# A linear-attention and token-mixer kernel: in the second batch both K projections come before the outputs, Q's features lie in weights' homes, and the three parts of the weights' conversion are traced a block apart

## The chip, the cores and the metric

The kernel runs on one core of a Trainium2 chip. The metric is the time of one execution on the device in microseconds; lower is better. Three runs of the kernel before gave a median of 1150.87 us, from 1150.61 to 1150.98 us.

The engines are named as the profile names them: PE multiplies matrices, ACT and DVE work element by element on tiles, POOL does the 64-bit integer additions and the reductions over partitions, and SP issues the transfers between the chip's memory (HBM) and the on-chip memories SBUF and PSUM. [...] Each engine works through its own queue in order, and waits at an instruction until the semaphores that it names are set.

## The reference

Eight batches of eight heads with 576 rows of 64 numbers each go through linear attention with 128 features of each sign; the result, 576 rows of 512 numbers in each batch, goes through a mixer over rows (rank 32) and one over channels (512 to 2048 and back). The two weights w_ch1 and w_ch2, and U and V, come as 64-bit floating point; everything else is 32-bit.

```python
def phi(x):
    proj = np.einsum('bhsd,df->bhsf', x, w_phi)
    proj = proj - np.max(np.abs(proj), axis=-1, keepdims=True)
    return np.concatenate([np.exp(proj), np.exp(-proj)], axis=-1)
q_p, k_p = (phi(q), phi(k))
kv = np.einsum('bhsf,bhsd->bhfd', k_p, v)
z = np.sum(k_p, axis=2)
num = np.einsum('bhsf,bhfd->bhsd', q_p, kv)
den = np.einsum('bhsf,bhf->bhs', q_p, z)[..., None] + 1e-06
...
h = xt @ U @ V
u = x + h.transpose(0, 2, 1)
ch = np.maximum(u @ w_ch1, 0.0) @ w_ch2
return (u + ch).astype(np.float32)
```

## The kernel before

**Attention.** The heads are taken in pairs: a pair (b, j) is batch b and heads 2j and 2j+1, so there are four pairs in a batch. A pair's q and k are loaded (tiles `raw` for the 512 first rows, `t_r` for the last 64), transposed (`T`, `tail_T`), projected on the features (`pk` and `pkt` for K, `pq` and `pqt` for Q, all in PSUM), and turned into exponentials (`kp`, `kp_t`, `qp`, `qp_t`; `_t` marks the last 64 rows). `s_kv` sums K's features against v (`kv_ps`, then `kv`); `s_out` multiplies Q's features by that (`xpt`, `xp`) and divides, into `x` and, for the last 64 rows, `xt`. Batches 0 and 1 are transposed on PE, batches from 2 on by DVE. Three pairs are in flight: `cur` is at its outputs, `nxt` at its projections, `far` at its loading.

**Mixer.** Each batch has `pp`, `pst`, `vp` (the mixer over rows, into `x`), four transposes `pt` into `uT_hi` and `uT_lo`, and then 16 blocks of 128 hidden channels. Each block f has a first chunk, `hidden(f)` (12 matmuls into PSUM tile `ph`, then `h_hi` on ACT and `h_lo` on DVE), and a second chunk, `add(f)` (12 matmuls into `o`). `hidden(f+1)` stands ahead of `add(f)`. The chunks of one batch are laid between the attention steps of the next: each `pace.step()` emits one or two. The chunks of batch 0 thus run beside the attention of batch 1, which the change calls the second batch; it lies between about 90 and 235 us.

**The weights' conversion.** Each of the 16 blocks has two halves, one of w_ch1 and one of w_ch2, so there are 32 halves, numbered i. `load_weights` brings a block's 64-bit words, 0.5 MB for each half (`words`). `convert` makes 32-bit numbers of them: three operations on ACT (L143, L144, L146), a shift on DVE (L147) and an addition on POOL (L151), in one of four scratch buffers (`w_ab`). `split_w` then makes a leading part by a cast (L245; on ACT for w_ch1, on DVE for w_ch2) and a remainder by a subtraction on DVE (L246). `blocks(upto)` converts all halves up to a number, at every `pace.step()` by the line

```python
blocks(EARLY + steps[0] * (2 * NFC - EARLY) // CONVERT)
```

and at a chunk that needs a half which is still missing. It is needed for batch 0's chunks alone, since later batches find the weights converted. `made` holds the newest `h_hi`, behind which a conversion is placed by `issue_after`. Four blocks' converted weights (`STREAM`) are stored to HBM (`kept`) and read again by later batches.

**What sets the order.** PE's instructions stay in the order of the code. The other engines' and SP's queues are laid out by the framework, which places an instruction by a timeline of its own when it is traced; a conversion thus stands among the other work of ACT, DVE and POOL where that timeline had room. `LOADS` tells up to which block the weights are loaded with each of the first four pairs; `weights(LAST - 1)` and `weights(LAST)` load the rest. `q_features` lays Q's features of batch 0 and of pair (1,0) in SBUF homes of converted weights that do not exist yet (`w*_11`, `w*_12`).

## Time and profile before

| what | value |
|---|---|
| median of three runs | 1150.87 us |
| the profiled execution's own time | 1150.31 us |
| its span | 1148.5 us |
| mean granted clock of PE | 0.991 |
| ACT busy | 537.3 us, 47% |
| DVE busy | 672.1 us, 59% |
| POOL busy | 203.1 us, 18% |

The busy times are read from the first part of the page. The span is the time from the first to the last recorded instruction; the execution's own time is 1.8 us longer. The profile is one execution, so a sum made from its rows stands beside 1150.31 us, and the median of the runs is 0.56 us above that. In rows of the timeline, the number in square brackets is the idle time of that engine ahead of the row, with what ended it.

### The profile page before, as it was taken

To read this page: it belongs to the slowest core of one execution; us is meant where nothing else is said; L and a number is where in the kernel's file an instruction comes from. 1 tells how busy PE (TensorE), PEld (TensorE's weight loads), DVE (VectorE), ACT (ScalarE), POOL (GpSimd) and SP (SyncE) were. 2 spreads that over 40 slices of the span, in tenths; PEclk is the share of its full clock that TensorE was granted. 3 is DMA by queue.
4 is the path that set the end of the run, shared out by engine and by line. 5 is a ranking of instruction groups with operands and counts; after the bars stand their busy time and mean duration, and the time that the engine had idled before them with its cause. 6 is when DMAs were issued, how large, how long until landed. Compare 5 with 4: busy or idle time off the path is not lost.

```text
span 1148.5 us, 22126 instructions
## 1 busy us (share of the span) xinstructions
PE 1100.7 (96%) x8814; PEld 924.1 (80%) x8814; DVE 672.1 (59%) x1510; ACT 537.3 (47%) x1151; POOL 203.1 (18%) x154
## 2 busy tenths in 40 slices
PE   7877998899999999999999999999999999999998
PEld 6866876688887888888888888788888888888886
DVE  5767778656577656766667657765776434113111
ACT  6878787435553545354544554354535421111110
POOL 4434544201120112011111111011201200000000
PEclk8999999999999999999999999999999999999999
DMA  5995220322326233622353244413351126311101
GB/s 152 339 315 166 55 63 14 107 85 61 85 81 137 68 75 78 147 69 69 87 128 105 64 91 103 112 51 77 100 132 48 35 84 185 88 37 55 56 1 37
DMA packets 247047, 110.28 MB, mean 96 GB/s; under 512 B 211744, under 2 KB 224288, under 8 KB 246944
## 3 DMA queue, kind: packets, MB, share of 16 engines
q1 hardware_dynamic: 246624, 108.34, 35.7%
q8 instruction: 70, 1.15, 0.4%
q10 hardware_dynamic: 320, 0.52, 0.1%
q14 instruction: 33, 0.27, 0.1%
HBM read 86.80 MB, written 22.02 MB: 95 GB/s over the span
## 4 chain that ended last, share of the span: by engine, by line
PE 81%; DVE 6%; DMA 5%; ACT 4%; SPq 2%; issue 1%; POOL 1%; DVEq 0%; ACTq 0%; POOLq 0%
PE ph L77 31%; PE o L77 31%; PE kv_ps L77 6%; PE xp L77 4%; PE pq L77 3%; PE pk L77 2%; DMA words<-in_moe_w_ch_dram 2%; PE pp L77 1%; DVE w L246 1%; POOL w_ab L151 1%; DMA raw<-in_q_dram 1%; PE xpt L77 1%; PE vp L77 1%; DVE h_lo L688 1%; ACT w_ab L144 1%
## 5 line engine op out<-in xcount | busy, mean ns | idle before, releaser
L77 PE MATMUL ph<-uT_hi,w 128*128 128x512 f32 x1152 | 383.6, 394 | 6.0 <-DVE h_lo L688 6.0
L77 PE MATMUL o<-w,h_hi 128*128 128x512 f32 x1152 | 361.6, 395 | 0.0
L77 PEld LDWEIGHTS ph<-uT_hi,w 128*128 128x128 f32 x1152 | 216.3, 188 | 53.9 <-DVE h_lo L688 7.8
L77 PEld LDWEIGHTS o<-w,h_hi 128*128 128x128 f32 x1152 | 214.9, 189 | 45.1
L688 DVE SCALAR_TENSOR_TENSOR h_lo<-ph,h_hi 128x512 fp32r<-128x512 f32 x144 | 98.9, 687 | 244.0 <-ACT h_hi L687 243.4
L687 ACT ACTIVATE h_hi<-ph 128x512 fp32r<-128x512 f32 x144 | 85.6, 595 | 323.1 <-PE ph L77 322.8
L77 PE MATMUL o<-w,h_lo 128*128 128x512 f32 x576 | 225.9, 392 | 0.0
L77 PE MATMUL ph<-uT_lo,w 128*128 128x512 f32 x576 | 224.5, 390 | 0.0
L396 POOL PARTITION_ALL_REDUCE qp<-qp x64 | 128.5, 2014 | 247.4 <-ACT qp L395 247.4
L77 PEld LDWEIGHTS o<-w,h_lo 128*128 128x128 f32 x576 | 108.7, 189 | 23.3
L77 PEld LDWEIGHTS ph<-uT_lo,w 128*128 128x128 f32 x576 | 108.2, 188 | 20.9
L396 POOL PARTITION_ALL_REDUCE qp_t<-qp_t x32 | 25.7, 804 | 384.2 <-ACT qp_t L395 384.1
L348 DVE TENSOR_TENSOR T<-raw,T 64x512 fp32r<-64x512 f32 x96 | 70.9, 738 | 17.5 <-ACT T L347 15.0
L77 PE MATMUL kv_ps<-vb,kp 128*64 128x65 f32 x2048 | 68.5, 225 | 7.1 <-ACT kp L383 4.3
L77 PEld LDWEIGHTS kv_ps<-vb,kp 128*64 128x64 f32 x2048 | 63.4, 139 | 11.7 <-ACT kp L383 4.7
L398 ACT ACTIVATE qp<-qp 128x512 f32<-128x512 f32 x64 | 40.3, 630 | 66.1 <-DVE qp L397 65.9
L77 PE MATMUL xp<-kv,qp 128*64 128x65 f32 x2048 | 66.8, 224 | 3.9 <-ACT qp L399 3.7
L77 PEld LDWEIGHTS xp<-kv,qp 128*64 128x64 f32 x2048 | 63.8, 140 | 4.2 <-ACT qp L399 3.8
L347 ACT CAST T<-raw 64x512 fp32r<-64x512 f32 x96 | 59.3, 617 | 11.1 <-PE pq L77 9.9
L382 ACT ACTIVATE kp<-kp 128x512 f32<-128x512 f32 x64 | 40.4, 632 | 42.0 <-DVE kp L379 41.9
L151 POOL INT64_ADD w_ab<-w_ab x32 | 43.5, 1361 | 81.5 <-DVE w_ab L147 69.6
L397 DVE TENSOR_TENSOR qp<-qp 128x512 f32<-128x512 f32 x64 | 45.1, 705 | 19.3 <-POOL qp L396 18.9
(119 smaller groups left out, 1244.9 us busy)
## 6 DMA issues: line engine op xcount, KB each, us to landing
w<-kept SPq DMA_DIRECT2D x46, 512.0 KB, 3.7
words<-in_moe_w_ch_dram SPq DMA_DIRECT2D x32, 512.0 KB, 6.7
vb<-in_v_dram SPq DMA_DIRECT2D x64, 128.0 KB, 3.1
u_dram<-x SPq DMA_DIRECT2D x32, 256.0 KB, 2.9
st<-u_dram SPq DMA_DIRECT2D x16, 512.0 KB, 4.4
out_dram<-st SPq DMA_DIRECT2D x32, 256.0 KB, 2.1
y<-u_dram SPq DMA_DIRECT2D x56, 128.0 KB, 3.6
raw<-in_k_dram SPq DMA_DIRECT2D x96, 64.0 KB, 2.4
```

Source lines behind the costliest of these rows:

```text
L77: return tc.keep_in_program_order(nc.tensor.matmul(*args, **kw))
L144: nc.scalar.activation(out=bh.bitcast(F16)[:, :, 1], in_=f32(st[:, :, 1]), func=AF.Copy, scale=2.0 ** -60)
L151: nc.gpsimd.int64_add(a64, a64, b64)
L246: nc.vector.tensor_sub(w[:, 1, :], r, f32(w[:, 0, :]))
L347: nc.scalar.copy(out=m[here, s, :], in_=x_[here])
L348: nc.vector.tensor_sub(m[there, s, :], x_[here], f32(m[here, s, :]))
L382: nc.scalar.activation(out=kp[:, :, 0:F], in_=kp[:, :, F:2 * F], func=AF.Exp)
L396: nc.gpsimd.partition_all_reduce(qp[:, 0, :], qp[:, 1, :], P, ReduceOp.absmax)
L397: nc.vector.tensor_sub(qp[:, 1, :], qp[:, 1, :], qp[:, 0, :])
L398: nc.scalar.activation(out=qp[:, 0, :], in_=qp[:, 1, :], func=AF.Exp)
L687: on_act = nc.scalar.activation(out=h_hi, in_=ph, func=AF.Relu)
L688: on_dve = nc.vector.scalar_tensor_tensor(out=h_lo, in0=ph, scalar=0.0, in1=f32(h_hi), op0=ALU.max, op1=ALU.subtract)
```

## The change

It touches the first 240 us, up to the end of the second batch; from the third batch on, three small clearing instructions are left out and nothing else is moved.

- **Conversion.** `convert` is divided: `scale_words` (the three ACT operations), `add_words` (shift and addition), and `split_block` (cast and subtraction). `blocks` now takes one step at a time: it splits what is added, scales the next half, and adds the half before it. `CONVERT` goes from 21 to 24, so that the last halves come with later steps; what a chunk needs is completed by `splits(need)`.
- **Loads.** `LOADS` is (2, 4, 6, 8, 10) for five pairs, in place of (2, 5, 8, 10) for four. Blocks 11 to 15 are loaded behind the pairs' own loads, in three places.
- **Q's features.** Those of pairs (1,1) and (1,2) lie in the homes `w*_12` and `w*_14`.
- **K's projections.** For pairs (1,2) and (1,3), `s_project_k1` (the second K projection, and Q's for the last 64 rows) comes before `s_out` instead of behind it, and a bare `pace.step()` stands in its old place.
- **Small things.** `convert_uv` is called later in the first turn. `xt` is one tile for all batches, so its clearing (L938) at the end of every second batch is left out.

```diff
     def convert(st, name):
+        return add_words(*scale_words(st, name))
+
+    def scale_words(st, name):
...
         nc.scalar.activation(out=f32(a), in_=f32(st[:, :, 1]), func=AF.Abs, scale=2.0 ** -112)
+        return a, b_
+
+    def add_words(a, b_):
+
         nc.vector.tensor_scalar(
             out=a, in0=a, scalar1=3, scalar2=None, op0=ALU.logical_shift_left)
...
-    def convert_block(i):
+    def scale_block(i):
         f, n = divmod(i, 2)
-        r = convert(words[f][n], f"w{n + 1}_{f}")
+        found[i] = scale_words(words[f][n], f"w{n + 1}_{f}")
+
+    def add_block(i):
+        found[i] = add_words(*found[i])
+
+    def split_block(i):
+        f, n = divmod(i, 2)
         if f not in WHOLE:
             w = home.tile([P, 2, C], F32R, tag=f"w{n + 1}_{f}", name=f"w{n + 1}_{f}")
-            split_w((nc.scalar.copy, nc.vector.tensor_copy)[n], r, w)
+            split_w((nc.scalar.copy, nc.vector.tensor_copy)[n], found.pop(i), w)
...
-            if m == SM and (self.b == 0 or self.b == 1 and self.h0 == 0):
-                f = 11 + self.h0 // 2 % 2
+            lent = {0: (11, 12, 11, 12), 1: (11, 12, 14)}.get(self.b, ())[self.h0 // 2:]
+            if m == SM and lent:
+                f = lent[0]
...
-    loaded, converted = [0], [0]
+    loaded, scaled, added, ready = [0], [0], [0], [0]
...
-    def blocks(upto):
-        while converted[0] < min(upto, 2 * NFC):
+    def up_to(at, fn, upto):
+        while at[0] < min(upto, 2 * NFC):
             with ExitStack() as order:
 
                 for ins in made[-1:]:
                     for i in ins:
                         order.enter_context(tc.issue_after(i.ins))
-                convert_block(converted[0])
-            converted[0] += 1
+                fn(at[0])
+            at[0] += 1
+
+    def splits(upto):
+        up_to(added, add_block, upto)
+        up_to(ready, split_block, upto)
+
+    def blocks(upto):
+        while scaled[0] < min(upto, 2 * NFC):
+            splits(added[0])
+            up_to(scaled, scale_block, scaled[0] + 1)
+            up_to(added, add_block, scaled[0] - 1)
...
-                    blocks(2 * f + (2 if f == LAST or fn.__name__ == "add" else 1))
+                    need = 2 * f + (2 if f == LAST or fn.__name__ == "add" else 1)
+                    blocks(need)
+                    splits(need)
...
             mix(n)
+            splits(added[0])
...
-    LOADS = (2, 5, 8, 10)
-    EARLY, CONVERT = 5, 21
+    LOADS = (2, 4, 6, 8, 10)
+    EARLY, CONVERT = 5, 24
...
-        weights(LAST - 1)
+        with tc.issue_after(far.loaded.ins):
+            weights(11)
...
-        weights(LAST)
...
+            close = n > NPAIR + 2
             if nxt is not None and nxt.kp0 is None:
                 nxt.s_project_k0()
             pace.step()
+            if not close:
+                nxt.s_project_k1()
             pace.step()
             step(cur.s_out, x, xt)
-            if nxt is not None:
+            if not close:
+                with tc.issue_after(far.loaded.ins):
+                    weights((13, LAST)[n - NPAIR - 1])
+                pace.step()
+            elif nxt is not None:
                 step(nxt.s_project_k1)
...
-                    if b % 2 == 1:
-                        xt = moe.tile([P, C], F32, tag="xt", name=f"xt{b + 1}")
-                        nc.vector.memset(xt[ST:P], 0.0)
```

In the listings below the numbers at the ends of names are running numbers of tiles, and line numbers of the changed kernel are 12 to 13 higher than those of before at the same statement.

**SP, ahead of the loads of pair (1,1).** Before, this stands in SP's queue between the loads of pair (1,0) and the `t_r` of pair (1,1):

```order
59 L220 DMA words_1_738<-in_moe_w_ch_dram 128x4x256
60 L223 DMA words_2_739<-in_moe_w_ch_dram 128x1024
61 L316 DMA vb_91<-in_v_dram 128x4x64
62 L220 DMA words_1_742<-in_moe_w_ch_dram 128x4x256
63 L223 DMA words_2_743<-in_moe_w_ch_dram 128x1024
64 L220 DMA words_746<-in_moe_w_ch_dram 128x4x256
65 L223 DMA words_746<-in_moe_w_ch_dram 128x1024
66 L242 DMA kept_104<-w_0_723 128x1024
67 L305 DMA t_r_1_941<-in_k_dram 64x2x64
```

In the change the same place reads:

```order
53 L227 DMA words_1_728<-in_moe_w_ch_dram 128x4x256
54 L230 DMA words_2_729<-in_moe_w_ch_dram 128x1024
55 L328 DMA vb_91<-in_v_dram 128x4x64
56 L227 DMA words_1_732<-in_moe_w_ch_dram 128x4x256
57 L230 DMA words_2_733<-in_moe_w_ch_dram 128x1024
58 L317 DMA t_r_1_924<-in_k_dram 64x2x64
59 L304 DMA raw_1_0_920<-in_k_dram 128x2x256
60 L304 DMA raw_1_1_922<-in_q_dram 128x2x256
61 L317 DMA t_r_1_924<-in_q_dram 64x2x64
```

Counted from the loads of pair (1,0), 16 halves of words and one store to `kept` stood ahead of that `t_r` before, and 8 halves stand there now; block 8's words, the early ones of blocks 13 and 14, and the store are behind it.

**ACT, around `hidden(6)` of the second batch.** Before, these rows stand between `h_hi` of block 6 and of block 7:

```order
232 L687 ACTIVATE h_hi_6_1962<-ph_6_1949 128x512
233 L143 ACTIVATE w_9_ab<-words_2_949 128x512
234 L144 ACTIVATE w_9_ab<-words_2_949 128x512
235 L146 ACTIVATE w_9_ab<-words_2_949 128x512
236 L383 ACTIVATE kp_3_0_1903<-kp_3_0_1903 128x4x128
237 L245 CAST w_9_1946<-w_9_ab 128x512
238 L687 ACTIVATE h_hi_7_2055<-ph_7_2042 128x512
```

In the change, with `kp_3_1` the second K features of pair (1,3) and `qp_3_t` its Q features for the last rows:

```order
226 L394 ACTIVATE kp_3_1_1912<-kp_3_1_1912 128x4x128
227 L700 ACTIVATE h_hi_6_1945<-ph_6_1932 128x512
228 L146 ACTIVATE w_8_ab<-words_935 128x512
229 L395 ACTIVATE kp_3_1_1912<-kp_3_1_1912 128x4x128
230 L147 ACTIVATE w_8_ab<-words_935 128x512
231 L149 ACTIVATE w_8_ab<-words_935 128x512
232 L408 COPY qp_3_t<-pqt_3_1918 128x128
```

The K features stand ahead of block 6's `h_hi` now, the conversion there is at block 8 instead of 9, and the copy that empties `pqt`'s PSUM tile stands behind that conversion. On PE, `pqt_3` itself has moved from behind `hidden(7)` to just ahead of `hidden(6)`, and `xp_1_2`, the outputs of pair (1,2), come behind `hidden(6)` as before.

**ACT, ahead of the last block.** Before, between `h_hi` of blocks 14 and 15:

```order
334 L687 ACTIVATE h_hi_14_2728<-ph_14_2715 128x512
335 L382 ACTIVATE kp_1_0_2699<-kp_1_0_2699 128x4x128
336 L383 ACTIVATE kp_1_0_2699<-kp_1_0_2699 128x4x128
337 L687 ACTIVATE h_hi_15_2757<-ph_15_2744 128x512
```

In the change:

```order
327 L700 ACTIVATE h_hi_14_2706<-ph_14_2693 128x512
328 L146 ACTIVATE w_15_ab<-words_2046 128x512
329 L147 ACTIVATE w_15_ab<-words_2046 128x512
330 L149 ACTIVATE w_15_ab<-words_2046 128x512
331 L395 ACTIVATE kp_1_0_2677<-kp_1_0_2677 128x4x128
332 L146 ACTIVATE w_15_ab<-words_2046 128x512
333 L147 ACTIVATE w_15_ab<-words_2046 128x512
334 L149 ACTIVATE w_15_ab<-words_2046 128x512
335 L257 CAST w_2739<-w_15_ab 128x512
336 L700 ACTIVATE h_hi_15_2757<-ph_15_2744 128x512
```

And what DVE has behind `h_lo` of block 14 in the change:

```order
347 L701 SCALAR_TENSOR_TENSOR h_lo_14_2707<-ph_14_2693,h_hi_14_2706 128x512
348 L154 TENSOR_SCALAR w_14_ab<-w_14_ab 128x512
349 L154 TENSOR_SCALAR w_15_ab<-w_15_ab 128x512
350 L257 CAST w_14_2728<-w_14_ab 128x512
351 L258 TENSOR_TENSOR w_14_2728<-w_14_ab,w_14_2728 128x512
352 L154 TENSOR_SCALAR w_15_ab<-w_15_ab 128x512
353 L258 TENSOR_TENSOR w_2739<-w_15_ab,w_2739 128x512
354 L257 CAST w_2739<-w_15_ab 128x512
355 L258 TENSOR_TENSOR w_2739<-w_15_ab,w_2739 128x512
356 L701 SCALAR_TENSOR_TENSOR h_lo_15_2758<-ph_15_2744,h_hi_15_2757 128x512
```

The whole conversion of block 15, which was over by 211 us before, has moved between the last two `hidden` chunks. On PE only `add(13)` stands between those two.

## Prediction

> **What bounds the kernel now.** I read the engines' busy time first, then PE's waits in the first 260 us, since the change touches nothing behind 240 us but three clearings.

> ```profile
> PE 1100.7 (96%) x8814; PEld 924.1 (80%) x8814; DVE 672.1 (59%) x1510; ACT 537.3 (47%) x1151; POOL 203.1 (18%) x154
> ...
> PE tT L80 <- DMA t_r<-in_q_dram: 5.4, 2, 4.5
> ```

> The lower row gives an engine, the tile at which it waited, what it waited for, the total, the count and the longest wait in us. PE is busy for 96% of the span, and PE's work is the same before and after: the same rows, two pieces of them moved. So the time changes only where PE waits, and by the clock after a wait. The longest wait of the front ends on a transfer, and those of the second batch, which stand with their terms below, end on ACT or DVE. Two stretches show which engines are full there.

> ```profile
> 45.00:60.00 15.00, 12.01 (x184) 11.00 (x185) 10.24 (x29) 14.17 (x32) 6.81 (x6) 1.00 1.07 351
> 165.00:180.00 15.00, 9.68 (x67) 7.89 (x68) 13.00 (x21) 12.33 (x24) 8.75 (x6) 0.97 0.32 59
> ```

> The columns are the stretch, its length, the busy time of PE, PE's weight loads, DVE, ACT and POOL, the granted clock, the share of the DMA engines and GB/s. Up to 60 us the transfers are saturated; from 165 to 180 us PE is busy for 9.68 of 15 us beside DVE at 13.00 and ACT at 12.33. There, where a conversion stands in ACT's and DVE's queues decides what PE waits for.

> **The front: a gain.** The longest wait is for the `t_r` of pair (1,1).

> ```profile
> 63.13 0.63 SPq L305 DMA_DIRECT2D t_r<-in_q_dram  x1
> 70.26 0.45 PE L80 MATMUL tT<-ident,t_r 128*128 128x128 f32 x1 [4.47 <-DMA t_r<-in_q_dram]
> 70.50 1.91 PE L80 MATMUL T<-ident,raw 128*128 128x128 f32 x8
> 72.21 1.07 PE L77 MATMUL kv_ps<-vt,kp_t 128*128 128x130 f32 x4
> 96.82 1.04 PE L80 MATMUL T<-ident,raw 128*128 128x128 f32 x8
> 130.15 0.61 PE L77 MATMUL kv_ps<-vt,kp_t 128*128 128x130 f32 x4
> ```

> Eight halves and one store less stand ahead of these loads on SP. A half is 0.524 MB, 1.5 us at the 351 GB/s above, so they land some 9 x 1.5 = 13 us earlier, well ahead of the 65.8 us at which PE is ready (70.26 less 4.47). What goes is 4.47 of waiting, 0.87 in the eight transposes (1.91 against 1.04) and 0.46 in the next four matmuls (1.07 against 0.61): 5.8. What is late next are the splits of x on ACT and DVE that `pp` and `vp` need; they had lain in the shade of that wait. I give 0.6 back: **-5.2**, bounds -5.9 and -4.5.

> **Prices on ACT, DVE and POOL.** The rest comes from the order in these queues and from these rows.

> ```profile
> 108.71 0.64 ACT L398 ACTIVATE qp<-qp 128x512 f32<-128x512 f32 x1
> 109.24 0.62 ACT L382 ACTIVATE kp<-kp 128x512 f32<-128x512 f32 x1
> 109.76 0.61 ACT L245 CAST w<-w_ab 128x512 fp32r<-128x512 f32 x1
> 110.27 0.31 ACT L383 ACTIVATE kp_t<-kp_t 128x128 f32<-128x128 f32 x1
> 110.48 0.59 ACT L687 ACTIVATE h_hi<-ph 128x512 fp32r<-128x512 f32 x1
> 110.96 0.77 ACT L143 ACTIVATE w_ab<-words 128x512 uint16<-128x512 uint16 x1
> 111.59 0.76 ACT L144 ACTIVATE w_ab<-words 128x512 f16<-128x512 f32 x1
> 112.21 0.65 ACT L146 ACTIVATE w_ab<-words 128x512 f32<-128x512 f32 x1
> 112.75 0.63 ACT L399 ACTIVATE qp<-qp 128x512 f32<-128x512 f32 x1
> ...
> L246 DVE TENSOR_TENSOR w<-w_ab,w x28: 648/691/1728, 95.2 to 210.7; 128x512 fp32r<-128x512 f32 x28
> L151 POOL INT64_ADD w_ab<-w_ab x27: 1266/1292/1652, 96.6 to 208.4; - x27
> L147 DVE TENSOR_SCALAR w_ab<-w_ab x26: 396/420/1503, 100.8 to 207.9; 128x512 int32<-128x512 int32 x26
> L245 DVE CAST w<-w_ab x14: 412/428/1386, 99.6 to 209.7; 128x512 fp32r<-128x512 f32 x14
> ```

> On ACT, start to start, an exponential costs 0.53, a cast 0.51, a small exponential 0.21, an `h_hi` 0.48, and a half's three scalings 1.79 (110.96 to 112.75). On DVE a subtraction takes 0.69, a shift and a cast 0.42 each, on POOL an addition 1.29.

> **A new wait at `xp_1_2` (G).** This output goes to the PSUM bank that the copy of `qp_3_t` empties; before, that bank was filled only later. The stretch of PE from the end of `hidden(5)` to this output was:

> ```profile
> 140.49 0.38 PE L77 MATMUL pkt<-w_f,tail_T 128*128 128x128 f32 x2
> 141.38 0.81 PE L77 MATMUL o<-w,h_hi 128*128 128x512 f32 x2
> 147.40 2.04 PE L77 MATMUL xp<-kv,qp 128*64 128x65 f32 x64
> ```

> That is 6.9 us, and the second K projection with the small Q one, about as long as the first (140.49 to 141.38, 0.9), now stand in it: 7.8. ACT, from `h_hi_5` on, must do that `h_hi` 0.48, two halves 3.58, five exponentials, a cast and two small exponentials 3.58, then `h_hi_6` 0.48, three scalings with an exponential among them 2.32, and the small copy 0.27: 10.7 us. The difference, 2.9, is new; I take a little less, since an exponential may find its input early: **+2.7**, bounds 1.9 (two exponentials less) and 3.2.

> **Removed wait B and old waits A, C, D, E.**

> ```profile
> 113.43 1.04 PE L77 MATMUL xp<-kv,qp 128*64 128x65 f32 x28 [3.69 <-ACT qp L399]
> 115.84 1.05 PE L77 MATMUL o<-w,h_hi 128*128 128x512 f32 x2
> 134.37 0.62 PE L77 MATMUL o<-w,h_hi 128*128 128x512 f32 x2
> 166.33 1.04 PE L77 MATMUL kv_ps<-vb,kp 128*64 128x65 f32 x28 [2.10 <-ACT kp L383]
> 178.04 0.41 PE L77 MATMUL pkt<-w_hl,tail_T 128*128 128x128 f32 x2 [3.98 <-DVE tail_T L325]
> 207.78 0.34 PE L77 MATMUL kv_ps<-vb,kp 128*64 128x65 f32 x4 [2.88 <-ACT kp L382]
> 209.94 1.79 PE L77 MATMUL kv_ps<-vb,kp 128*64 128x65 f32 x28 [1.82 <-ACT kp L383]
> ```

> B, the 2.10 at 166 us, goes: the K features of pair (1,3) now stand ahead of `h_hi_6`, more than a block early: **-2.1**.

> A, the 3.69, stays. Its `xp` now waits for a division on DVE that stands behind `h_lo_2`, and ACT reaches `h_hi_2` 8.2 us after `h_hi_1` (0.48, two halves 3.58, and six exponentials, two small ones and a cast 4.1), against 7 to 7.5 us of PE: 3.1 to 4.9 in place of 3.69, so -0.6 to +1.2, taken as **+0.3**. Behind it the copy of `qp_2_1` stands behind three halves on ACT instead of two, 1.79 more, part of it covered: 0 to 1.2, **+0.6**. Block 8's first weights come as late as `hidden(8)`: 0 to 1.2, **+0.3**.

> C, the 3.98 for `tail_T`, stays. Its last copy on ACT now stands behind `h_hi_9` and four scalings of blocks 11 and 12: 0.48 + 1.79 + 0.6 and the copy and DVE's share of it, 0.8, are 3.7 us after `hidden(9)` at the least. With every DVE subtraction on the way stretched it is 7.3: 0 to +3.3, taken nearer to the plain rows, **+1.5**. D, a small wait for the copy of `qp_t` near 199 us, loses 0 to 0.8 by the same queue, **+0.4**. E, 4.70 in two pieces, stands behind blocks 13 and 14 on ACT as it stood behind 14 and 15: 3.7 to 5.8, -0.9 to +1.1, **+0.1**.

> **A new wait at the last block (F).** Only `add(13)` stands on PE between `hidden(14)` and `hidden(15)`, 2.8 us by the twelve matmuls of the chunk in the rows below (229.45 to 232.30). The whole of block 15 is converted there. Counted from the end of `hidden(14)`: `h_hi` and `h_lo` to 1.4, the shift of `w_14`'s second half to 1.8, its addition to 3.1, cast and subtraction to 4.2; this frees the scratch buffer that block 15's second half waits for; its scalings run to 6.1, and the cast and the subtraction of the first half, behind them in ACT's and DVE's queues, to 7.3. PE waits 7.3 - 2.8 = 4.5. The wait at the same place before goes with its cause.

> ```profile
> 225.55 0.48 DVE L938 MEMSET xt<- 64x512 f32 x1 [4.37 <-DMA u_dram<-xt]
> 229.45 0.50 PE L77 MATMUL ph<-uT_hi,w 128*128 128x512 f32 x1 [0.83 <-DVE h_lo L688]
> 232.30 1.47 PE L80 MATMUL pt<-ident,x 128*128 128x128 f32 x12
> ```

> The clearing waited 4.37 us for a transfer and made `h_lo` late, 0.83 on PE. So 4.5 - 0.8 = **+3.7**; bounds 2.9 (the buffer free 0.9 earlier) and 4.9 (one subtraction stretched). The other two clearings have no wait behind them: 0. PE's slow clock after the wait is a term of its own. After 3.69 a pair of `o` matmuls took 1.05 instead of 0.62, for four such pairs, some 1.6 us in all with the single ones; after 2.10 and below nothing is seen. For 4.5 that is 0 to 1.6, **+0.8** taken as the middle, since the transposes behind `hidden(15)` have slack.

> [...]

> **The sum.** -5.2 + 2.7 - 2.1 + 0.3 + 0.6 + 0.3 + 1.5 + 0.4 + 0.1 + 3.7 + 0.8 = **+3.1**. On the profiled execution's 1150.3 that is 1153.4, and by its 0.56 below the median, **1154.0**: slower by 0.27%. All low ends give -4.7 (1146), all high ends +11.9 (1163).

> **Rivals.**

> *The lag works, and the kernel is faster.* The casts wait for POOL now.

> ```profile
>   ACT w L245: 4.9, 5
>   DVE w L245: 8.6, 6
> ```

> The rows are who waited for an addition between 95 and 235 us, how long and how often. With cast and subtraction a block behind, those 4.9 us on ACT go. If all of it reaches PE at A, C and E instead of my +1.9 there, the sum is 3.1 - 1.9 - 4.9 = -3.7, 1147; if also the queue ahead of the last block is one half shorter (1.8 less at F), 1145. It decides from where ACT's lost time stands ahead of those waits and neither DVE nor the end of a `ph` is later; five waits of 1 us, over 140 us, seldom stand so. 0.18.

> *The last block isn't late.* If `w_15` is converted ahead of `hidden(14)` after all, F and its clock go: 1154.0 - 4.5 = 1149.5, no change. Against it stands the order on ACT. 0.14.

> *The load gain fails.* If the loads of pair (1,1) are held by another tile than the queue, the 5.2 stay: 1159.2. The saturated DMA share speaks for little of that. 0.07.

> *Subtractions meet additions.* One beside an addition took long:

> ```profile
> 107.11 1.67 DVE L246 TENSOR_TENSOR w<-w_ab,w 128x512 fp32r<-128x512 f32 x1
> 106.92 1.32 POOL L151 INT64_ADD w_ab<-w_ab  x1 [0.51 <-DVE w_ab L147]
> ```

> 1.67 is 0.98 over the median. With the parts apart, a subtraction stands beside the next half's addition more often; one at each of A, C, E and F makes +3.9, 1157.9. 0.16. [...]

> **How the numbers follow.** My forecast has 0.45, between 1149.5 and 1157. A measurement of this kernel can tell some 0.2% (2.3 us) from no change: below 1148.6 is faster, above 1153.2 slower. Faster: 0.16 of the first rival, 0.04 of the second, 0.07 of the forecast, 0.27. Slower: 0.07 and 0.15 of the last two, 0.23 of the forecast, 0.01 of the second: 0.46. The rest is 0.27. For 8 in 10 the range reaches into the first rival and over the last two: 1145 to 1160.

> **What would show it.** PE should wait for no `t_r` near 65 us, and its first `ph` should come at 88 to 89 us instead of 93.75. A wait of 2 to 3 us should stand at an `xp` behind `hidden(6)`, none at `kv_ps` after it, and one of 3 to 5 us at the last `ph` of the second batch, ended by a subtraction on DVE. The forecast is wrong if the waits for `tail_T` and for the last K features are gone: then ACT's and DVE's queues hold less than I counted.

## The result, and the profile after

The changed kernel takes 1162.38 us (median of four runs, 1162.31 to 1163.85) beside 1150.74 us for the kernel before in the same runs: a ratio of 1.0107, with a 95% interval of 1.009 to 1.0125. The forecast was 1154.0 us in a range of 1145 to 1160: the direction is right, and the loss is 11.6 us where 3.1 were forecast.

Where it lies is read from three stretches of each execution: up to the first `ph` of the first mixer, from there to the first `ph` of the next one, and the rest. These are the rows of before, with the columns as in the prediction (stretch, its length, busy time of PE and of the others, clock, DMA share, GB/s).

```profile
0.00:93.75 93.75, 74.20 (x989) 63.47 (x990) 65.43 (x177) 67.95 (x154) 36.30 (x46) 0.95 0.86 269
93.75:239.58 145.83, 128.64 (x930) 106.55 (x928) 107.28 (x204) 105.01 (x207) 57.59 (x40) 0.96 0.25 66
239.58:1148.50 908.92, 897.89 (x6899) 754.03 (x6897) 499.36 (x1130) 364.35 (x791) 109.21 (x69) 1.00 0.33 83
```

And these are the same stretches of the changed kernel.

```profile
0.00:90.44 90.44, 75.75 (x989) 65.20 (x990) 65.49 (x174) 66.90 (x152) 36.59 (x45) 0.92 0.78 244
90.44:252.06 161.62, 133.52 (x930) 109.68 (x929) 111.51 (x207) 106.14 (x209) 60.09 (x41) 0.90 0.29 79
252.06:1160.60 908.54, 897.54 (x6899) 754.43 (x6897) 498.36 (x1128) 364.01 (x791) 109.26 (x69) 1.00 0.33 83
```

The counts of matmuls agree, so the stretches hold the same work. The third is unchanged. In the front PE waits 14.7 us (90.44 - 75.75) instead of 19.6, and is busy 1.6 us longer for the same 989 matmuls: 3.3 gained. In the second batch it waits 28.1 instead of 17.2 and is busy 4.9 us longer: 15.8 lost. Of the whole difference of 12.1 us in the span, **6.0 are waiting and 6.1 are the same matmuls at a lower clock** (mean granted clock 0.981, before 0.991).

The waits in PE's timeline, at the places that the prediction named A, G, C, D, E and F (start, duration, engine, line, operation, and the idle time ahead with its end):

```profile
110.10 1.15 PE L77 MATMUL xp<-kv,qp 128*64 128x65 f32 x32 [3.06 <-DVE xt L507]
147.21 1.15 PE L77 MATMUL xp<-kv,qp 128*64 128x65 f32 x32 [2.10 <-ACT qp_t L408]
159.57 0.74 PE L77 MATMUL ph<-uT_hi,w 128*128 128x512 f32 x2 [1.48 <-DVE w L258]
178.38 0.66 PE L77 MATMUL pkt<-w_hl,tail_T 128*128 128x128 f32 x2 [7.09 <-DVE tail_T L337]
200.78 1.22 PE L77 MATMUL pq<-T,w_hl 128*128 128x512 f32 x2 [2.03 <-ACT qp_t L408]
210.31 0.34 PE L77 MATMUL kv_ps<-vb,kp 128*64 128x65 f32 x4 [1.58 <-ACT kp L394]
213.63 1.78 PE L77 MATMUL kv_ps<-vb,kp 128*64 128x65 f32 x28 [2.98 <-ACT kp L395]
238.33 0.79 PE L77 MATMUL ph<-uT_hi,w 128*128 128x512 f32 x1 [5.63 <-ACT w L257]
240.08 1.22 PE L77 MATMUL ph<-uT_hi,w 128*128 128x512 f32 x2 [0.53 <-DVE w L258]
```

Each wait stands where the prediction put it: the new one at `xp` behind `hidden(6)` (2.10), none at `kv_ps` behind it, block 8's weights (1.48), `tail_T` (7.09, before 3.98) and the last block (5.63 and 0.53, before 0.83). The two in the chunk of block 15 come from these rows of DVE, in which a conversion's shift is L154, its cast L257 and its subtraction L258:

```profile
232.61 0.97 DVE L154 TENSOR_SCALAR w_ab<-w_ab 128x512 int32<-128x512 int32 x1 [0.78 <-ACT w_ab L149]
233.50 0.41 DVE L257 CAST w<-w_ab 128x512 fp32r<-128x512 f32 x1
233.95 1.63 DVE L258 TENSOR_TENSOR w<-w_ab,w 128x512 fp32r<-128x512 f32 x1
237.60 0.43 DVE L154 TENSOR_SCALAR w_ab<-w_ab 128x512 int32<-128x512 int32 x1 [2.02 <-ACT w_ab L149]
238.31 1.72 DVE L258 TENSOR_TENSOR w<-w_ab,w 128x512 fp32r<-128x512 f32 x1 [0.28 <-ACT w L257]
```

and from these of ACT (the row that waits for DVE) and POOL:

```profile
235.67 0.78 ACT L146 ACTIVATE w_ab<-words 128x512 uint16<-128x512 uint16 x1 [2.58 <-DVE w L258]
...
232.02 1.28 POOL L158 INT64_ADD w_ab<-w_ab  x1 [11.52 <-DVE w_ab L154]
233.75 1.28 POOL L158 INT64_ADD w_ab<-w_ab  x1 [0.45 <-DVE w_ab L154]
238.20 1.28 POOL L158 INT64_ADD w_ab<-w_ab  x1 [3.17 <-DVE w_ab L154]
```

The subtraction at 233.95 frees the scratch buffer; it began 0.2 us behind an addition on POOL and took 1.63 instead of 0.69, so ACT started the last half's scalings at 235.67, 0.9 later than without. The next subtraction, at 238.31, met an addition too, which is the second wait of 0.53.

### The profile page after: what moved, and what is told of

Same layout as the page of the kernel before. It is cut to its first block, busy times and chain, and to the rows that moved or that the text cites. A ratio compares the mean times of both kernels' runs of the same rounds, so it can differ in the third digit from the quotient of the medians.

```text
span 1160.6 us, 22131 instructions
## 1 busy us (share of the span) xinstructions
PE 1106.8 (95%) x8814; PEld 929.3 (80%) x8814; DVE 675.4 (58%) x1507; ACT 537.0 (46%) x1151; POOL 205.9 (18%) x154
## 3 DMA queue, kind: packets, MB, share of 16 engines
q8 instruction: 70, 1.15, 0.4%
## 4 chain that ended last, share of the span: by engine, by line
PE 85%; DVE 6%; ACT 5%; SPq 1%; DMA 1%; issue 1%; POOL 1%; ACTq 0%; POOLq 0%; DVEq 0%
PE ph L77 32%; PE o L77 32%; PE kv_ps L77 6%; PE xp L77 5%; PE pq L77 3%; PE pk L77 3%; PE pp L77 1%; DVE w L258 1%; PE xpt L77 1%; ACT w_ab L146 1%; PE vp L77 1%; ACT w_ab L147 1%; ACT h_hi L700 1%; DVE h_lo L701 1%; ACT w_ab L149 1%
## 5 line engine op out<-in xcount | busy, mean ns | idle before, releaser
L77 PE MATMUL ph<-uT_hi,w 128*128 128x512 f32 x1152 | 386.8, 397 | 12.7 <-ACT w L257 5.6
L77 PE MATMUL o<-w,h_hi 128*128 128x512 f32 x1152 | 360.8, 395 | 0.0
L77 PEld LDWEIGHTS ph<-uT_hi,w 128*128 128x128 f32 x1152 | 217.9, 189 | 61.4 <-ACT w L257 6.1
L77 PEld LDWEIGHTS o<-w,h_hi 128*128 128x128 f32 x1152 | 214.6, 189 | 44.7
L77 PE MATMUL ph<-uT_lo,w 128*128 128x512 f32 x576 | 226.2, 393 | 0.0
L77 PE MATMUL o<-w,h_lo 128*128 128x512 f32 x576 | 225.6, 392 | 0.0
L77 PEld LDWEIGHTS o<-w,h_lo 128*128 128x128 f32 x576 | 108.7, 189 | 23.3
L77 PEld LDWEIGHTS ph<-uT_lo,w 128*128 128x128 f32 x576 | 109.2, 190 | 21.1
L77 PE MATMUL xp<-kv,qp 128*64 128x65 f32 x2048 | 68.5, 227 | 5.6 <-DVE xt L507 3.1
L77 PE MATMUL kv_ps<-vb,kp 128*64 128x65 f32 x2048 | 68.2, 225 | 4.7 <-ACT kp L395 3.1
L77 PEld LDWEIGHTS kv_ps<-vb,kp 128*64 128x64 f32 x2048 | 63.3, 139 | 9.0 <-ACT kp L395 3.4
L77 PEld LDWEIGHTS xp<-kv,qp 128*64 128x64 f32 x2048 | 65.3, 143 | 6.0 <-ACT w_ab L149 3.2
```

The costliest lines, as they stand in the source:

```text
L77: return tc.keep_in_program_order(nc.tensor.matmul(*args, **kw))
```

## The experiments

Each kernel was timed against the kernel before on the same chip; ratios are to that, with their 95% intervals. The changed kernel's own ratio is 1.0107 (1.009 to 1.0125), and 0.1% is 1.15 us.

| kernel | what differs from the change | ratio (95%) |
|---|---|---|
| c21 | CONVERT 21 | 0.9968 (0.9949 to 0.9986) |
| c23 | CONVERT 23 | 0.9926 (0.9905 to 0.9947) |
| nolag | no lag between the parts | 0.9979 (0.9967 to 0.9992) |
| nolag21 | no lag, CONVERT 21 | 1.0004 (0.9991 to 1.0017) |
| nolag23 | no lag, CONVERT 23 | 0.9939 (0.9924 to 0.9953) |
| loads_only | no lag, CONVERT 21, K's projection late | 0.9958 (0.9945 to 0.9972) |
| k1late_c21 | CONVERT 21, K's projection late | 0.9970 (0.9957 to 0.9983) |
| nolag23_k1late | no lag, CONVERT 23, K's projection late | 0.9916 (0.9885 to 0.9947) |
| oldloads_c21 | CONVERT 21, loads and homes of before | 1.0042 (1.0026 to 1.0059) |
| gate | conversion placed behind `tail_T` | 1.0044 (1.0028 to 1.0059) |
| busy | useless matmuls in one wait | 1.0076 (1.0058 to 1.0094) |
| fill | useless matmuls in three waits | 1.0066 (1.0051 to 1.0081) |

**The pace and the lag.** The first question was which of the two puts the conversion late.

```diff
-    EARLY, CONVERT = 5, 24
+    EARLY, CONVERT = 5, 21
```

> The change with CONVERT at 21 again, so that block 15's halves are scaled at earlier steps; all else as in the change. Theory P (pace): the late pace alone puts block 15 between the last two hidden chunks, and of the 12 us lost some 8 are the wait there (5.6 and 0.5, less 0.8 before) and the slow clock behind it; expected: a wait of at most 1.5 us at the last ph, no slow matmuls there, 1153 to 1156 us. Theory L (lag): the parts of the conversion that are traced a block apart are what is late, at every block; expected: the casts and subtractions still come late, at most 3 us gained, over 1159 us.

Measured: 0.9968, the wait at the last `ph` gone, and a mean granted clock of 0.987 in the profiled execution, in the change 0.981. That is theory P, but the gain of some 16 us (1.4%) is about twice what it gave. Read at the starts of the same `ph` tiles, the last block is 9.5 us of it; 7 us more come earlier, 4.7 of them between the starts of blocks 9 and 10, where the wait for `tail_T` is 3.30 instead of 7.09.

```diff
     def blocks(upto):
         while scaled[0] < min(upto, 2 * NFC):
-            splits(added[0])
             up_to(scaled, scale_block, scaled[0] + 1)
-            up_to(added, add_block, scaled[0] - 1)
+            splits(scaled[0])
```

> The change with each half scaled, added and split at one step, CONVERT still 24. Theory P: block 15 is still converted between the last two hidden chunks, wait there 4 to 7 us and slow matmuls behind; within 4 us of the change, 1158 to 1163 us. Theory L: the waits for tail_T (7.1), qp_t (2.0) and the last ph go back to those of before; below 1154 us.

Measured: 0.9979, against both expectations in part. Theory P had it within 4 us of the change; it gained 15. Theory L had the last wait go; it stays, at 2.92 us, with slow matmuls behind:

```profile
225.30 0.79 PE L77 MATMUL ph<-uT_hi,w 128*128 128x512 f32 x1 [2.92 <-ACT w L257]
225.89 0.63 PE L77 MATMUL ph<-uT_lo,w 128*128 128x512 f32 x1
```

Without the lag block 14's second half is split ahead of `h_hi` of block 14, so its buffer is free, and the last wait is half as long. The wait for `tail_T` is 4.52 instead of 7.09, the one for block 8's weights is gone, and those for `kp` are 2.12 instead of 4.56 (at D it waits 2.28 instead of 2.03). So the lag and the pace each do most of the harm only beside the other.

The kernel with both edits, CONVERT 21 and no lag:

> The change with each half converted at one step and CONVERT at 21, so that the loads, the homes of Q's features and K's order are all that is left of it. Theory P and theory L both: the conversion is as before, so the wait at the last ph is under 1 us; what is left is the front (-3.3), the removed wait for kp (-2.1) and the new one at xp (+2.1): 1146 to 1150 us. If the order of K's projections or the loads were what costs, it stays above 1155 us.

Measured: 1.0004, above the 1146 to 1150 us that was expected. The wait at the last `ph` is gone, as expected, but at `xp` PE waits 4.37 and 3.35 us, more than in the change (3.06 and 2.10). That K's early projection is what costs more there, with the conversion ahead again, is shown by the later run loads_only, which takes that projection out and leaves the rest.

One number apart from the change, and the sharpest test of its pace:

```diff
-    EARLY, CONVERT = 5, 24
+    EARLY, CONVERT = 5, 23
```

> The change with CONVERT 23 in place of 24 and nothing else: the last half is scaled with the last step of the second batch, ahead of hidden(13). Theory P (the pace of one number puts block 15 between the last two chunks): no wait over 1 us at the last ph and no slow clock behind it, which were worth 9 us; the waits at tail_T (7.1) and qp_t (2.0) are a matter of how many halves are still left there and shrink by 0 to 3 us: 1.000 to 1.003 of before. Theory L (it is the lag): the casts of block 15 still come behind h_hi of block 14; over 1.006 of before.

Measured: 0.9926, better than expected: 1.8% by one number, by the two ratios (18.7 us between the profiled executions). There are 23 steps in the second batch, so at 24 the last two halves are left for the last chunk, which must complete them at once. By the starts of the same `ph` tiles 9.5 of 18.8 us lie at the last block and 8.2 at the wait for `tail_T`:

```profile
172.96 0.41 PE L77 MATMUL pkt<-w_hl,tail_T 128*128 128x128 f32 x2 [1.38 <-DVE tail_T L337]
...
223.22 0.39 PE L77 MATMUL ph<-uT_hi,w 128*128 128x512 f32 x1
```

The last `ph` has no idle time ahead of it. That `tail_T` waits 1.38 instead of 7.09 was not expected of the pace. ACT's order shows how: with 23 both copies of `tail_T` stand ahead of `h_hi` of block 9.

```profile
171.06 0.24 ACT L336 CAST tail_T<-tT 64x128 fp32r<-64x128 f32 x1
172.22 0.26 ACT L336 CAST tail_T<-tT 64x128 fp32r<-64x128 f32 x1 [0.92 <-DVE tail_T L337]
172.51 0.60 ACT L700 ACTIVATE h_hi<-ph 128x512 fp32r<-128x512 f32 x1
```

In the change the second copy stands behind `h_hi`, and DVE's second subtraction for it follows a long one beside POOL:

```profile
172.15 0.59 ACT L700 ACTIVATE h_hi<-ph 128x512 fp32r<-128x512 f32 x1
...
173.62 0.28 DVE L337 TENSOR_TENSOR tail_T<-tT,tail_T 64x128 fp32r<-64x128 f32 x1
...
173.89 0.64 ACT L149 ACTIVATE w_ab<-words 128x512 f32<-128x512 f32 x1
174.43 0.77 ACT L146 ACTIVATE w_ab<-words 128x512 uint16<-128x512 uint16 x1
175.22 0.26 ACT L336 CAST tail_T<-tT 64x128 fp32r<-64x128 f32 x1
...
175.81 1.77 DVE L258 TENSOR_TENSOR w<-w_ab,w 128x512 fp32r<-128x512 f32 x1
177.50 0.41 DVE L154 TENSOR_SCALAR w_ab<-w_ab 128x512 int32<-128x512 int32 x1
177.94 0.29 DVE L337 TENSOR_TENSOR tail_T<-tT,tail_T 64x128 fp32r<-64x128 f32 x1
```

Here the copy at 175.22 comes 3.1 us behind `h_hi`, past four scalings. It waits for DVE's first subtraction, as the row at 172.22 above shows, and that ended at 173.90: so of the 3.1 us the scalings cost it 1.3, from 173.90 on. DVE reaches the second subtraction at 177.94, 2.5 us after the copy's end. Beside c23, where neither takes any time, and with the first subtraction 2.0 us later in the chunk of block 9, that makes the 5.7 us more. The next run forces the other order on the change, by placing each piece of the conversion behind the newest `tail_T`:

```diff
-            nc.vector.tensor_sub(dst[D:2 * D], src, f32(dst[0:D]))
+            gate[:] = [nc.vector.tensor_sub(dst[D:2 * D], src, f32(dst[0:D]))]
...
                     for i in ins:
                         order.enter_context(tc.issue_after(i.ins))
+                for i in gate:
+                    order.enter_context(tc.issue_after(i.ins))
                 fn(at[0])
```

> The change with each scaling and split of the conversion placed behind the newest subtraction of tail_T, so that both copies of tail_T stand ahead of h_hi of block 9 and of the scalings of blocks 11 and 12 on ACT. Theory Q (the wait of 7.1 us for tail_T is made by these scalings and by the split beside POOL's addition): that wait is at most 3 us, and 4 us or more of it stay gained up to hidden(10); the last block stays late (5 to 6 us); 1.003 to 1.008 of before. Rival: T's own splits on DVE end as late; the wait stays over 5 us and the time at 1.009 or more; or the conversion behind the gate is what comes late instead, at ph of block 10.

Measured: 1.0044, and

```profile
172.80 0.65 PE L77 MATMUL pkt<-w_hl,tail_T 128*128 128x128 f32 x2 [2.05 <-DVE tail_T L337]
...
180.40 0.74 PE L77 MATMUL ph<-uT_hi,w 128*128 128x512 f32 x2 [1.86 <-DVE w L258]
```

The wait falls from 7.09 to 2.05, which theory Q expected; 1.86 of it come back at block 10, whose weights are now behind the gate, which the rival named. At the start of block 11 some 4 us are kept (187.9 against 192.2 in the change), of which 0.5 were there before block 9. Another 3.9 us come between the starts of blocks 12 and 13, at the waits for `kp`, and no run tells why. The last block stays late, at 5.66 us.

**Loads and K's order.** These take the other parts of the change alone.

```diff
-            if not close:
-                nxt.s_project_k1()
             pace.step()
...
                     weights((13, LAST)[n - NPAIR - 1])
-                pace.step()
+                step(nxt.s_project_k1)
```

> The change with CONVERT 21 and with the second K projections of pairs (1,2) and (1,3) behind the outputs again. Theory G: the waits of xp behind hidden(2) and hidden(6) (2.1 and 1.6 us there) are set by the banks that the earlier projection fills, so they shrink by 1 to 3 us together, and a wait of some 2 us at kv_ps is back; in sum within 2 us of the change with CONVERT 21. Rival: the early projection is what makes that one fast; over 3 us slower.

Measured: 0.9970 beside 0.9968, in sum as theory G expected. The `xp` waits shrink from 2.13 and 1.59 to 0.39 and nothing, and a wait at `kv_ps` of 3.46 us comes. It is an exchange of more waits than these: two of 1.78 and 1.11 us come at `pp`, and that of 3.30 for `tail_T` goes.

With this edit, CONVERT 21 and no lag, the loads and homes remain alone:

> The kernel before with the new loads and homes alone (and without the clearings): each half converted at one step, CONVERT 21, K's second projection behind the outputs. Theory F: no wait for t_r, first ph at 90.5 to 92 us, the second batch as before: 2 to 4 us under before, 0.9965 to 0.9985. Rival: splits of x on ACT and DVE end the front as late as the loads did; within 1 us of before.

Measured: 0.9958, 4.8 us under before, somewhat more than the 2 to 4 of theory F. The first `ph` comes at 91.5 us, as expected; the waits of the second batch (3.69 at `xp`, 2.07 at `kv_ps`, 3.98 for `tail_T`, 2.92 and 1.82 for `kp`) are those of before to 0.05 us, and only the 0.83 at the last `ph` is missing with the clearing. So this part of the change is a gain by itself. Beside nolag21 (1.0004), which differs by K's early projection, it shows that projection to cost 0.46%, 5 us, at this pace.

Its counterpart puts the loads of before into c21. It also takes the homes of Q's features from pairs (1,1) and (1,2), since those homes hold words again.

```diff
-    LOADS = (2, 4, 6, 8, 10)
+    LOADS = (2, 5, 8, 10)
...
-        with tc.issue_after(far.loaded.ins):
-            weights(11)
+        weights(LAST - 1)
...
-            lent = {0: (11, 12, 11, 12), 1: (11, 12, 14)}.get(self.b, ())[self.h0 // 2:]
+            lent = {0: (11, 12, 11, 12), 1: (11,)}.get(self.b, ())[self.h0 // 2:]
```

> The change with CONVERT 21 and with the loads of the kernel before: LOADS (2, 5, 8, 10), blocks 11 to 14 and then 15 where they were, and Q's features of pairs (1,1) and (1,2) in their own tiles again. Theory F (the loads' order is worth the front's gain): the wait of about 4.5 us for t_r of pair (1,1) is back, the first ph comes at 93 to 95 us instead of 90.8, and the time is 2 to 4 us over that of the change with CONVERT 21 (0.997 of before): 0.999 to 1.001 of before. Rival: what comes late next takes the gain anyhow; within 1 us of it.

Measured: 1.0042, some 8 us over c21 where 2 to 4 were expected, and for other reasons than expected: the wait for `t_r` is back at 1.58 us only and the first `ph` comes at 91.35 us. In this run SP has no store to `kept` ahead of that `t_r` and issues it at 60.96 us, before at 63.13, and PE is ready for it 1.1 us later; so the order of the words alone doesn't make the 4.47 us of before. The loss is in the second batch, with 3.05 us at `xp` behind `hidden(6)`. Which of loads and homes it is can't be told from this run. Its times spread widely (1152.9 to 1159.8), and the profile is of one of the fastest (1153.14).

**The best of these.** With a pace that leaves nothing for the last chunk (CONVERT 23) and the edit of nolag:

> The change with each half converted at one step and CONVERT 23, so that the last half comes with the last step of the second batch and none is left for the last chunk. Theory P: the wait of 2.9 us at the last ph and the slow clock behind it (some 5 us with CONVERT 24 and no lag) go: 0.9935 to 0.9965 of before. Rival: what is converted earlier makes the waits at xp, tail_T and kp longer, as with CONVERT 21: 0.998 to 1.001.

Measured: 0.9939, as theory P expected.

With K's projection behind the outputs too:

> The loads and homes of the change, each half converted at one step, CONVERT 23, and K's second projection behind the outputs. If the early projection still costs its wait at xp behind hidden(6) (2.0 us with it), and the wait at kv_ps that it removes is 2 to 3.5 us: within 2 us of the same kernel with the early projection (0.994 of before), 0.993 to 0.996. Rival: the early projection is worth more there; over 0.997.

Measured: 0.9916, under the 0.993 to 0.996 that was expected, with a wide interval. It and c23 (0.9926) are the fastest, 8 to 10 us under before, and K's order makes no difference at this pace that these runs can tell.

**The clock.** Does PE lose speed because it was idle? These put matmuls without use, on a constant, into waits of the change.

```diff
                     splits(need)
+                    if f == LAST and fn.__name__ == "hidden":
+                        wp = ps("busy", "ph")
+                        for _ in range(20):
+                            mm(wp, v_all[:, 0:P], v_all[:, 0:512], start=True, stop=True)
                 fn(f)
```

> The change with 20 matmuls more on PE (128x512, a constant with itself, the result used by nobody) ahead of the last hidden chunk of the first mixer, where PE waits 5.6 us. Theory C (the clock falls when PE is idle): the matmuls fill 4.5 us of the wait, the clock stays at full speed behind it, and the 3 us that the next chunks lost there are gone: 1158.5 to 1160.5 us with as long a wait in all. Rival: the slow matmuls there have another cause (what ACT, DVE and POOL do at that time): no gain, 1162 to 1164 us.

Measured: 1.0076, 3.6 us less than the change by the ratios, whose intervals just overlap; the profiled executions differ by 2.5. The last block's `ph` in its profile:

```profile
232.06 4.70 PE L77 MATMUL busy<-v_all 128*128 128x512 f32 x20
237.94 0.50 PE L77 MATMUL ph<-uT_hi,w 128*128 128x512 f32 x1 [1.18 <-ACT w L257]
238.28 0.39 PE L77 MATMUL ph<-uT_lo,w 128*128 128x512 f32 x1
239.69 0.73 PE L77 MATMUL ph<-uT_hi,w 128*128 128x512 f32 x2 [1.02 <-DVE w L258]
240.26 0.39 PE L77 MATMUL ph<-uT_lo,w 128*128 128x512 f32 x1
```

and in the change's:

```profile
238.92 0.63 PE L77 MATMUL ph<-uT_lo,w 128*128 128x512 f32 x1
```

The weights come no earlier, and each matmul is fast (0.39 instead of 0.63). From the end of `add(13)` to the first `pt` it is 9.9 us, in the change 11.8. So the slow matmuls behind this wait come from PE being idle in it, not from what the other engines do.

Run fill does it at three waits, with `fill(8)` at the start of pair (2,0)'s `s_project_k0` and `s_project_q0` and `fill(20)` ahead of the last `hidden`; `fill` is the loop above.

> The change with matmuls of no use (128x512, a constant with itself) ahead of three of PE's waits: 8 ahead of pkt (wait of 7.1 us for tail_T), 8 ahead of the pq at 200 us (2.0 us), 20 ahead of the last ph (5.6 us). No wait is made shorter. Theory C (half clock for one stretch of 3.41 us after a stretch with some 1.9 us or more of idle PE, ends of all slow stretches being at one phase of 3.41 us): the slow chunks behind all three go, which cost about 0.9 or more, 1.6 and 2.8 us; 1.0107 of before becomes 1.005 to 1.0075. Rival: the slow matmuls come from load on other engines; 1.009 or more.

Measured: 1.0066, at a mean granted clock of 0.987 in the profiled execution, in the change 0.981. By an estimate from these two, 0.006 of some 1160 us is 7 us of clock, so some 14 us fewer are spent at 0.50. The slow stretch behind D is gone:

```profile
199.73 0.73 PE L77 MATMUL pq<-T,w_hl 128*128 128x512 f32 x2 [0.20 <-ACT qp_t L413]
200.29 0.40 PE L77 MATMUL ph<-uT_hi,w 128*128 128x512 f32 x1
```

while the change, behind its 2.03 us at the same place, has

```profile
201.80 0.63 PE L77 MATMUL ph<-uT_hi,w 128*128 128x512 f32 x1
```

Part of the gain is lost again by the start of block 13: waits of 0.86 and 0.27 us come at `pp`, and the slow stretch at the waits for `kp` (211.6 to 218.5 us, in the change 211.0 to 217.8) holds 5.9 us of matmuls instead of 4.2. The time is within theory C's range, but the two intervals overlap, so it can't be told from that of busy.

## Why the prediction was wrong, step by step

- **The front.** Forecast -5.2, measured -3.3 (93.75 to 90.44). The wait for `t_r` went as said, and by the stretches above waiting fell by 4.9, more than the 3.9 in the sum (4.47 less 0.6). But the sum also counted 1.3 us for slow matmuls that would go, and PE's busy time became 1.6 more: waits of 1.71, 0.65 and 0.41 us at `vp` and `xp` are followed by such matmuls (clock 0.50 from 77.88 to 84.70 us), and so is one of 2.62 at 46 us, which stood there before too, with nothing slow behind it (the rows are below).
- **B** went: -2.1 forecast, and no wait stands there. From the start of `kv_ps` to that of the `pq` behind it are 2.6 us (161.96 to 164.52), before 4.9 (162.42 to 167.30).
- **G** came true in mechanism and size: 2.7 forecast, 2.10 waited, ended by the copy of `qp_t` that the prediction named.
- **A** was said to stay at 3.1 to 4.9 and was 3.06, ended by the division named, so -0.6 for the +0.3 taken. Its slow stretch, which the sum left in its place, went: a pair of `o` matmuls behind it takes 0.62, before 1.05. The copy of `qp_2_1` behind A, 0.6 taken: 0.84 us, at a transpose.
- **Block 8's weights**: 0.3 taken of 0 to 1.2, 1.48 measured. The subtraction that ends this wait met an addition (157.67 to 158.97):

```profile
157.75 1.77 DVE L258 TENSOR_TENSOR w<-w_ab,w 128x512 fp32r<-128x512 f32 x1
```

- **D**: 0.4 taken, 0.9 of waiting measured and a slow `hidden(12)` behind it (single matmuls of 0.63 us, 0.39 in run fill), which the sum had not. **E**: 0.1 taken, -0.1 measured.
- **C** was taken "nearer to the plain rows" at +1.5, which is 5.5 us; it was 7.09, near the end of 7.3 "with every DVE subtraction on the way stretched". The order on ACT was the one named, but the rows beside c23 give the scalings only 1.3 of 5.7 us; the rest is mostly on DVE, whose share was put at less than 0.8. The run gate shows that 5.0 of the 7.09 hang on where the conversion stands.
- **F** was the right mechanism: block 15 between the last two chunks, the scratch buffer, the two halves. 4.5 us of waiting were forecast and 6.16 measured, as two subtractions met additions, not at most one, and the longer wait ended with the cast on ACT, not with a subtraction. (By the rows that the prediction names, 0.9 earlier and one stretched subtraction give bounds of 2.8 and 4.7, not 2.9 and 4.9.) c23 shows that the whole of it hangs on CONVERT.
- **The rival with subtractions beside additions** had a chance of 0.16 and proved right at C and F and, where it didn't look, at block 8, but not at A and E; its price of 1 us each is what the rows show (1.77, 1.77, 1.63 and 1.72 for 0.69).

The waits in the forecast add to +3.6 us and measured +6.0. The step that failed most is the clock: "after 2.10 and below nothing is seen", so that only the wait at the last block got a price, 0.8, against 1.3 gained in the front. The forecast for the clock was thus -0.5, and it is +6.1. The length of a wait didn't decide it. These are a wait of before and the same one in the changed kernel, with the matmuls behind each:

```profile
47.13 0.46 PE L77 MATMUL pkt<-w_f,tail_T 128*128 128x128 f32 x2 [2.63 <-ACT tail_T L367]
47.43 1.89 PE L77 MATMUL pk<-w_two,T 128*128 128x256 f32 x8
```

```profile
46.46 0.46 PE L77 MATMUL pkt<-w_f,tail_T 128*128 128x128 f32 x2 [2.62 <-ACT tail_T L379]
46.76 3.22 PE L77 MATMUL pk<-w_two,T 128*128 128x256 f32 x8
```

The traces of before and of the change show what went with it. From 12 us on their granted clock is 1.00 or 0.50, and the times at which it changes lie whole multiples of 3.41 us apart within each execution. Up to 250 us it was 0.50 in before for 3.41 us each from 18.76, 25.59, 69.96, 114.33, 179.19 and 209.91 us; in the change for 3.41 us each from 26.68, 47.16 and 200.76, for 6.83 us each from 77.88 and 211.00, and for 10.24 us each from 173.45 and 234.89. Between 12 and 250 us 120 such periods of 3.41 us begin at 1.00 in the two traces. The 107 in which PE was idle for 1.72 us or less were followed by another at 1.00, and the 13 in which it was idle for 1.82 us or more by one at 0.50. In the traces of the twelve runs five periods between 12 and 86 us went otherwise: four with some 1.5 us idle, near 77 us, were followed by a slow one, and one with 1.94 us by a fast one; why is open. So in the traces of before and of the change it is the idle time within one period that tells what follows, and a wait that is divided between two periods did less. The wait of 2.63 us at 47.13 in before is divided, with 1.56 and 1.07 us of idle PE in two periods, and no slow one follows (1.00 in both rows, and up to 69.96 us). That of 2.62 us in the change lies in one, and the next has half the clock (0.50). First before, then the change:

```profile
42.65:46.07 3.42, 1.85 (x64) 1.71 (x60) 2.93 (x7) 3.42 (x9) 0.67 (x1) 1.00 1.09 327
46.07:49.48 3.41, 2.35 (x12) 2.14 (x13) 2.15 (x6) 3.37 (x9) 1.27 (x1) 1.00 1.06 343
```

```profile
43.75:47.16 3.41, 0.79 (x8) 0.71 (x5) 1.56 (x5) 3.37 (x9) 0.00 (x0) 1.00 1.01 312
47.16:50.57 3.41, 3.41 (x9) 2.70 (x9) 2.32 (x5) 2.27 (x7) 0.00 (x0) 0.50 1.10 349
```

These rows of the change are one period each too, two at A and two at D; the third number from the end is the granted clock:

```profile
105.19:108.60 3.41, 1.84 (x42) 1.35 (x41) 2.92 (x10) 3.41 (x8) 0.00 (x0) 1.00 0.11 21
108.60:112.01 3.41, 1.91 (x36) 1.74 (x37) 3.21 (x9) 3.41 (x8) 2.33 (x2) 1.00 0.42 138
197.35:200.76 3.41, 1.40 (x7) 0.89 (x5) 2.65 (x6) 3.34 (x10) 2.44 (x2) 1.00 0.04 10
200.76:204.17 3.41, 3.39 (x8) 2.71 (x9) 3.35 (x5) 1.76 (x5) 2.72 (x3) 0.50 0.04 10
```

A's 3.06 us are divided, 1.57 and 1.50 us of idle PE with the small gaps, and nothing slow follows. D's 2.03 us lie in one period, which is idle for 2.01, and the next has half the clock (0.50). In before A's 3.69 us left 2.51 us idle in the period from 110.92, and the next was slow. That A's slow stretch went is thus, by these rows, a matter of where its wait fell among the periods.

An estimate of what each place holds: in the change single `ph` matmuls start 0.43 us apart at a clock of 0.50 (201.80 to 202.23) and 0.23 at 1.00 (205.21 to 205.44), so I take half of PE's busy time in a slow period as its cost. By that A holds -1.7 us against before, C +1.0, D +1.7, E +0.4 and F +3.1, together 4.5 of the 4.9 us of the second batch. F alone was given a price, and a fourth of this one.

What stays open: what of oldloads_c21 is loads and what homes; why the periods of the two executions lie at different phases (the first at 0.50 begin at 18.76 us and at 26.68 us, 2.3 periods apart); and what filling or shortening one wait does to the slow stretches behind it, since it moves them.

## What to carry to other kernels

When conversions are spread over steps, count the steps that there are, and let the spread end with the last one: CONVERT 24 over 23 steps left a whole block for the last chunk and cost 1.8% beside CONVERT 23 by the ratios, together with what it shifted. Ending earlier was no better here (CONVERT 21: 0.9968, 23: 0.9926). A wait had a second price on PE here: in the traces of before and of the change each period of 3.41 us from 12 to 250 us that began at a clock of 1.00 and in which PE was idle for 1.82 us or more was followed by one at half the clock, which by the estimate above costs up to 1.7 us. When a sum is made along queues whose DVE and POOL parts meet, take a longer duration for each subtraction that the order puts beside an addition: of the conversion's 32 subtractions in the change's trace 13 began while POOL was at an addition, and 11 of these took 0.86 to 1.77 us; the other 21 took 0.68 or 0.69.

## What the runs showed of the hardware that was not expected

A shift with one input on DVE took 0.97 us instead of 0.42 beside an addition on POOL (the row at 232.61 with the addition that runs from 232.02). In the change's trace 6 of the conversion's 32 shifts took 0.83 to 1.25 us, and all six began while POOL was at an operation; the other 26 took 0.41 to 0.43, and none of them did. So it is not the two-input subtractions alone that took longer there.
